# Seven products for half of an early first layer, and a transfer moved behind gathers, in an attention and expert-routing kernel

## The chip, the cores and the metric

One core of a Trainium2 chip runs the whole kernel. Its engines are TensorE (matmuls, PE in the profile), VectorE (DVE), ScalarE (ACT), GpSimd (POOL) and SyncE (SP, which here only issues transfers). The metric is the device time in microseconds of one execution, as the median of several; lower is better.

## The reference

Attention over blocks of 64 positions with a decaying state, then a routing layer in which each of 3072 tokens goes to one of 8 experts:

```python
batch, n_heads, seq, head_dim = (4, 8, 768, 64)
intra = einsum('bhic,bhjc->bhij', qb, kb) * Dmask        # per block of 64
out[:, :, sl] = einsum('bhij,bhjd->bhid', intra, vb) + einsum('bhid,bhde->bhie', qb * lam_pow, kv_state)
kv_state = lam_block * kv_state + einsum('bhsd,bhse->bhde', kb_dec, vb)
...
N, D, E, F = (3072, 512, 8, 1024)      # x: the attention's output, one row of 512 per token
logits = x @ w_gate
expert_idx = argmax(logits, axis=1)
gate_w = softmax(logits) at expert_idx
for e in range(E):
    h = maximum(x[mask] @ w1[e], 0.0)       # 512 -> 1024
    out[mask] = gate_w[mask] * (h @ w2[e])  # 1024 -> 512
```

All of it is in 32-bit floats.

## The kernel before

**Attention** runs in 12 steps of 128 positions and two batch rows. Each step turns q and k (L241), multiplies them (L279), applies the decay (L286), forms the output (L305, L314) and the state, turns the output back into token rows (L376), stores these in DRAM (`xs`, L386) and computes the logits (L366). From the logits VectorE finds each token's expert and its place in that expert's list; GpSimd stores the places one batch row at a time (L467, an indirect DMA into `slots`).

**Experts** are passes. Expert 5 (`FIRST`) comes in two parts: pass "0a" takes its first 256 tokens (`EARLY`) from the first four of the six blocks of positions and starts while the last step of the attention still runs; pass "0b" takes its other 128. Then follow the other seven experts, the second pass with up to 418 tokens. For each pass a list is read, its token rows are gathered from `xs` by an indirect DMA from GpSimd (`fetch`, L527, one per 128 tokens), turned so that features lie on partitions (`xgT`), and taken through w1 and w2. The two parts of expert 5 are turned by TensorE (`turn`, L592). From the second expert on, ScalarE splits the rows into 16-bit halves (`split`, L575, `planes_q` and `planes_k`), SP issues transposing DMAs (L577), and ScalarE joins the turned halves to `xgT` (`join`, L585).

**The layers.** Pass 0a's first layer (`hidden`, L606) is plain: for each of 8 blocks of 128 hidden features 4 matmuls of 128x128 weights with 256 tokens, then a ReLU by ScalarE (L559). Its second layer (`outputs_early` and `form_early`, matmuls in `block`, L774) multiplies hT by w2 as a 2x2 matrix of blocks with seven products instead of eight (Strassen's method in Winograd's form): with sums s1 to s4 of blocks of hT (`left_of`, L752 to L755, tiles h_qT, h_kT, h_sd, h_kd) and t1 to t4 of blocks of w2 (`second_sums`, L683, tiles t_q, t_k, t_v, t_m), both by VectorE, and u2, u3, u4 as running sums of products. Pass 0b has a plain first layer (128 tokens) and a second layer of seven products in halves of the array (`lone_tile`, L782, its adds L819 to L832). From the second expert on both layers use seven products (`hidden_fast`, L728, with sums of w1 by GpSimd in `first_sums`, L655 and L652, and sums of xgT by VectorE in `token_sums`, L713; `outputs_across`, L914).

**What sets the order.** Each engine takes its instructions in the order written out by the program; a scheduler places those that aren't pinned (`pin`). An engine waits on semaphores at an instruction, and what stands behind that instruction waits with it. Products lie in 8 banks of the accumulator memory (`bank(i, ...)`): a product in a bank waits until the engine that read the previous product there has done so. Tiles come from pools with a few buffers for each name (`qkv`: 3, `work`: 2, `wpool`: 2); xgT and hT have one buffer each.

**Around the end of the attention** GpSimd gathers pass 0a (`gather_early`), then waits until TensorE has turned back the last logits (`hold`), stores the last six places, and then gathers 0b and the second expert. SP loads w2 of expert 5 behind the early gathers, the lists, and w1 of the second expert (`load_weights`). Two tiles of the old state are reused as space: `qs_room` has four parts, `x_room` two.

## Time and profile before

| | |
|---|---|
| median of 3 runs | 434.31 us (432.14 to 435.08) |
| profiled execution | 435.07 us, of it a span of 432.8 us |
| busy: PE, DVE, POOL, ACT | 421.3, 266.0, 257.5, 176.8 us |
| granted TensorE clock, mean | 0.997 |
| DMA | 83.49 MB, mean 193 GB/s |

Times in the trace count from the start of the span. A row of the timeline is start, length, engine, line, operation, output<-inputs, and in brackets the idle time ahead of it and what ended that. Lxxx is a line of the kernel. Each matmul in 32-bit floats stands in the trace as two records. The chain of waits follows the work that ended last back to its start; "issue" in it is time in which the engine waited for nothing that the profile shows. In the table by stages stand, after the stage and its length, the busy times of PE, PE's weight loads, DVE, ACT and POOL with their counts, the clock, the share of the DMA engines and GB/s.

### The profile page before, as it was taken

To read this page: it belongs to the slowest core of one execution; us is meant where nothing else is said; L and a number is where in the kernel's file an instruction comes from. 1 tells how busy PE (TensorE), PEld (TensorE's weight loads), DVE (VectorE), ACT (ScalarE), POOL (GpSimd) and SP (SyncE) were. 2 spreads that over 40 slices of the span, in tenths; PEclk is the share of its full clock that TensorE was granted. 3 is DMA by queue.
4 is the path that set the end of the run, shared out by engine and by line. 5 is a ranking of instruction groups with operands and counts; after the bars stand their busy time and mean duration, and the time that the engine had idled before them with its cause. 6 is when DMAs were issued, how large, how long until landed. Compare 5 with 4: busy or idle time off the path is not lost.

```text
span 432.8 us, 9573 instructions
## 1 busy us (share of the span) xinstructions
PE 421.3 (97%) x3699; PEld 393.9 (91%) x3699; DVE 266.0 (61%) x585; ACT 176.8 (41%) x319; POOL 257.5 (59%) x205
## 2 busy tenths in 40 slices
PE   8999999999999999999999999999999999999993
PEld 6888898888888897999999999999999999999972
DVE  6656656566766647686547757755575664775463
ACT  3366545555542423450554155245424605422221
POOL 5243457373344368777948757693885887749032
PEclk9999999999999999999999999999999999999998
DMA  9999989999985758976369857965975894753122
GB/s 174 211 245 229 220 213 213 233 193 249 292 283 149 265 105 234 325 246 237 52 139 190 332 76 157 319 179 112 299 246 81 196 384 80 153 186 56 20 83 63
DMA packets 164727, 83.49 MB, mean 193 GB/s; under 512 B 146019, under 2 KB 146063, under 8 KB 164672
## 3 DMA queue, kind: packets, MB, share of 16 engines
q1 hardware_dynamic: 155024, 63.21, 61.2%
q0 software_dynamic: 5712, 13.26, 10.2%
q10 hardware_dynamic: 3936, 6.31, 4.2%
q8 instruction: 31, 0.51, 0.5%
q14 instruction: 24, 0.20, 0.2%
HBM read 58.96 MB, written 13.09 MB: 166 GB/s over the span
## 4 chain that ended last, share of the span: by engine, by line
PE 87%; DMA 4%; issue 3%; ACT 2%; POOL 1%; SPq 1%; DVE 1%; POOLq 0%; ACTq 0%
PE p L728 30%; PE p L914 26%; PE sp L279 5%; PE ph L606 5%; PE op L314 4%; PE p L774 3%; DMA v_in<-in_v_dram 3%; PE cp L340 2%; PE tx L376 2%; PE tk L241 2%; PE tq L241 2%; PE op L305 2%; PE p L782 2%; PE lgT L366 1%; DMA xg<-xs,list_0a 1%
## 5 line engine op out<-in xcount | busy, mean ns | idle before, releaser
L533 POOL DMA_INDIRECT out_dram<-o_room,list x24 | 25.7, 1069 | 51.9 <-DMA decay<-planes_q 22.4
L286 DVE TENSOR_TENSOR mt<-sp,decay 128x512 f32<-128x512 f32 x48 | 30.1, 684 | 23.8 <-PE sp L279 18.6
L739 ACT ACTIVATE hT<-hT 128x418 f32<-128x418 f32 (+6 forms) x56 | 28.3, 521 | 34.1 <-DVE hT L736 31.2
L728 PE MATMUL p<-xgT,w1t 128*128 128x209 f32 (+6 forms) x224 | 41.4, 327 | 0.0
L728 PEld LDWEIGHTS p<-xgT,w1t 128*128 128x128 f32 x224 | 37.1, 189 | 0.8 <-issue 0.8
L618 ACT COPY u_qT<-p 128x418 f32<-128x418 f32 (+6 forms) x14 | 6.7, 479 | 69.5 <-PE p L728 69.5
L914 PE MATMUL p<-hT,w2t 128*128 128x209 f32 (+5 forms) x192 | 33.6, 328 | 0.0
L914 PEld LDWEIGHTS p<-hT,w2t 128*128 128x128 f32 x192 | 32.0, 189 | 0.0
L467 POOL DMA_INDIRECT slots<-entry,slot_i x24 | 23.8, 990 | 13.1 <-PE tl L391 5.9
L527 POOL DMA_INDIRECT xg<-xs,list x25 | 25.9, 1034 | 9.0 <-issue 6.1
L736 DVE TENSOR_TENSOR hT<-p,u_kd 128x418 f32<-128x418 f32 (+6 forms) x28 | 15.6, 559 | 21.0 <-PE p L728 21.0
L279 PE MATMUL sp<-qT,kT 64*128 64x128 f32 x384 | 27.5, 293 | 0.4 <-ACT kT L263 0.4
L279 PEld LDWEIGHTS sp<-qT,kT 64*128 64x128 f32 x384 | 24.3, 199 | 3.0 <-issue 2.0
L269 POOL TENSOR_TENSOR kd<-k_in,kdec 128x512 f32<-128x512 f32 x12 | 12.4, 1042 | 23.7 <-PE cp L340 11.9
L655 POOL TENSOR_TENSOR s_q<-w1t 128x1024 f32<-128x1024 f32 x7 | 16.5, 2363 | 16.6 <-DVE t_xT L713 14.6
L326 ACT COPY xT<-op 128x512 f32<-128x512 f32 x12 | 7.0, 585 | 36.9 <-PE op L314 33.8
L606 PE MATMUL ph<-xgT,w1t 128*128 128x256 f32 (+1 forms) x128 | 21.6, 328 | 0.0
L606 PEld LDWEIGHTS ph<-xgT,w1t 128*128 128x128 f32 x128 | 19.2, 191 | 1.7
L728 PE MATMUL p<-t_sd,w1t 128*128 128x209 f32 (+6 forms) x112 | 20.7, 327 | 0.0
L728 PE MATMUL p<-st,s_q 128*128 128x209 f32 (+6 forms) x112 | 20.7, 327 | 0.0
L652 POOL TENSOR_TENSOR w1t<-w1t 128x1024 f32<-128x1024 f32 x7 | 20.2, 2892 | 0.6
L728 PE MATMUL p<-t_xT,w1t 128*128 128x209 f32 (+6 forms) x112 | 20.6, 326 | 0.0
(252 smaller groups left out, 1093.9 us busy)
## 6 DMA issues: line engine op xcount, KB each, us to landing
w2t<-in_moe_w_dram SPq DMA_DIRECT2D x8, 2048.0 KB
w1t<-in_moe_w_dram SPq DMA_DIRECT2D x7, 2048.0 KB
xs<-x_room ACTq DMA_DIRECT2D x12, 512.0 KB
v_in<-in_v_dram SPq DMA_DIRECT2D x8, 512.0 KB
o_room<-qs_room SPq DMA_DIRECT2D x76, 48.0 KB
q_in<-in_q_dram SPq DMA_DIRECT2D x7, 512.0 KB
k_in<-in_k_dram SPq DMA_DIRECT2D x7, 512.0 KB
room<-in_q_dram SPq DMA_DIRECT2D x4, 512.0 KB
```

The lines of the kernel that those rows point to most:

```text
L241: pin(nc.tensor.transpose(t[:, i, b, :], src[:, b, h:h + 2, :], ident))
L279: m.scored = pin(nc.tensor.matmul(sp[u][:, i, b, :], lhsT=m.kT[s][halves[u], i, b, :], rhs=m.qT[s][halves[u], i, b, :], start=(i == 0 and ...
L286: nc.vector.tensor_mul(mt[:, u], sp[u], decay[:, u, s * HP // 2:(s + 1) * HP // 2].unsqueeze(2).to_broadcast(shp))
L314: pin(nc.tensor.matmul(out_at(m, b, u, hp), lhsT=m.v[:, b, 2 * hp + u, :], rhs=m.mt[hp // 2][:, u, hp % 2, b, :], start=(first and hp == 0 ...
L467: put = nc.gpsimd.indirect_dma_start(out=slots, out_offset=bass.IndirectOffsetOnAxis(ap=slot_i[:, i:i + 1], axis=0), in_=entry[:, n, bs[i] ...
L527: return nc.gpsimd.indirect_dma_start(out=dst, out_offset=None, in_=xs[:rows, :], in_offset=bass.IndirectOffsetOnAxis(ap=idx, axis=0))
L533: put = nc.gpsimd.indirect_dma_start(out=out, out_offset=bass.IndirectOffsetOnAxis(ap=idx, axis=0), in_=src, in_offset=None, bounds_check= ...
L606: nc.tensor.matmul(ph, lhsT=w1t[:, dc, fc * P:(fc + 1) * P], rhs=m.xgT[:, dc, :], start=(dc == 0), stop=(dc == DC - 1))
L652: return nc.gpsimd.tensor_tensor(out=o, in0=x, in1=y, op=ALU.add)
L728: nc.tensor.matmul(p[:, i, :], lhsT=lhs[:, dc, g, i * P:(i + 1) * P], rhs=rhs[:, dc, :], start=(dc == 0), stop=(dc == DH - 1))
L739: pin(nc.scalar.activation(outs[i][k], outs[i][k], ACT.Relu))
L914: nc.tensor.matmul(p[:, c, :], lhsT=lhs[:, f, c * P:(c + 1) * P], rhs=rhs[:, f, :], start=(f == 0), stop=(f == FC // 2 - 1))
```

## The change

Three things change between the end of the attention and the second expert.

*Pass 0a's first layer* (`hidden_early`). Hidden features 0 to 511 stay plain, 4 blocks of 4 matmuls with 256 tokens. Features 512 to 1023 become a 2x2 by 2x2 product: the weights' blocks have 256 input by 256 hidden features, the tokens' 256 by 128. Seven products of 4 matmuls (128x128 weights, 128 tokens). The four sums of w1 (`early_sums`, tiles e_q, e_k) are made by GpSimd right behind the early gathers, ahead of its last stores; the four sums of xgT (e_sd twice, st, e_xT) by VectorE ahead of the sums of w2, which are now interleaved with the adds of the products (`others`). ScalarE copies the first product out and applies the ReLUs. The third product is added onto the first in its bank.

*Pass 0a's second layer* (`outputs_early`). The same seven products in another order and with fixed banks: 7, 4, 5, 7, 4, 7, 4. The product a22 t4 comes third instead of last, the one of s4 last. The first product is copied out by ScalarE instead of VectorE. One of the two scatters is issued before the last product.

*Transfers.* The second expert's list is read before 0b's, its four gathers are issued before 0b's, and the load of its w1 waits until the second of these gathers has landed (`behind`). 0b's turned rows go to the third part of `qs_room` (`short_room`) instead of the xgT buffer.

```diff
-    def load_weights(e, later=None):
+    def load_weights(e, later=None, behind=None):
         w1t = wpool.tile([P, DC, F], F32, tag="w1", name="w1t")
-        nc.sync.dma_start(out=w1t, in_=pick(w1_r, e))
+        begun = nc.sync.dma_start(out=w1t, in_=pick(w1_r, e))
+        if behind is not None:
+            pin(begun)
+            tc.add_manual_dep(begun.ins, behind.ins.name, ...)
...
+    def early_sums(w1t):
+        w = w1t.rearrange("p (j d) (g i f) -> p i j d g f", j=2, g=2, i=2)
+        a = [[w[:, i, j, :, 1] for j in range(2)] for i in range(2)]
+        q, k = (qkv.tile([P, 2, DH, FH // 2], F32, tag=t, name=f"e_{t}") for t in "qk")
+        s1, s2, s3, s4 = q[:, 0], q[:, 1], k[:, 0], k[:, 1]
+        pin(pool_sub(s3, a[0][0], a[1][0]))
+        pin(pool_add(s1, a[1][0], a[1][1]))
+        pin(pool_sub(s2, s1, a[0][0]))
+        pin(pool_sub(s4, a[0][1], s2))
...
+    def hidden_early(m, w1t, a, others):
+        h = m.n // 2
+        m.hT = ffn.tile([P, FC, m.n], F32, tag="hT", name="hT", bufs=1)
+        for fc in range(FC // 2):
+            ph = bank(next(ph_banks), [P, m.n], "ph")
+            for dc in range(DC):
+                nc.tensor.matmul(ph, lhsT=w1t[:, dc, fc * P:(fc + 1) * P], rhs=m.xgT[:, dc, :],
+                                 start=(dc == 0), stop=(dc == DC - 1))
+            relu(1, m.hT[:, fc, :], ph)
...
+        x1 = product(a.a11, b.b11, 0)
+        pin(nc.scalar.copy(p1, x1))
+        x7 = product(a.s2, b.t2, 1)
+        ready(0, 0, product(a.a12, b.b21, 0, x1))
+        others.pop(0)()
+        add(u2, x7, p1)
+        x3 = product(a.s3, b.t3, 2)
+        others.pop(0)()
+        add(u3, x3, u2)
+        x6 = product(a.a22, b.t4, 3)
+        others.pop(0)()
+        add(outs[1][0], x6, u3)
+        ready(1, 0)
+        x5 = product(a.s1, b.t1, 6)
+        add(outs[1][1], x5, u3)
+        ready(1, 1)
+        add(u4, x5, u2)
+        others.pop(0)()
+        add(outs[0][1], product(a.s4, b.b22, 1), u4)
+        ready(0, 1)
...
+        for make in (a.s1_made, a.s2_made, a.s3_made, a.s4_made):
+            make()
+        nc.scalar.copy(p1, block(a.a11, b.b11, 7))
+        give(0, 0, block(a.a12, b.b21, 4), p1)
+        p6 = block(a.a22, b.t4, 5)
+        add(u2, block(a.s2, b.t2, 7), p1)
+        add(u3, block(a.s3, b.t3, 4), u2)
+        give(1, 0, p6, u3)
+        p5 = block(a.s1, b.t1, 7)
+        give(1, 1, p5, u3)
+        add(u4, p5, u2)
+        scatter(at(m, 1)[1], o[1])
+        ahead()
+        give(0, 1, block(a.s4, b.b22, 4), u4)
+        scatter(at(m, 0)[1], o[0])
...
         begun = fetch(m, 1 + (NSTEP - 2) * B * C, pin)
         hold(begun[0], other)
+        m.sums = early_sums(weights[0][0])
...
-    passes.append(make_pass(FIRST, EARLY, CAPS[0] - EARLY, "0b"))
     next_pass(1)
+    passes.insert(1, make_pass(FIRST, EARLY, CAPS[0] - EARLY, "0b"))
+    short_room = qs_room[:, 2].rearrange("p i b c -> p (i b) c")
     later = []
-    weights.append(load_weights(passes[2].w, later))
-    for m in passes[1:]:
-        fetch(m)
+    begun = fetch(passes[2], pin=pin)
+    fetch(passes[1], pin=pin)
+    weights.append(load_weights(passes[2].w, later, begun[1]))
```

On ScalarE, from the ReLUs of pass 0a to the copies that follow the split of the second expert's rows (`planes`), before:

```order
L559 ACTIVATE hT<-ph 128x256 x8
L575 COPY planes_q<-xg 128x512 x4
L575 COPY planes_k<-xg 128x512 x2
L575 COPY planes_k<-xg 48x512 x2
L599 COPY xgT<-tp 128x256
```

and now (`pe` are the products of the first layer's half, `x_room` holds the copy of the first product of the second layer):

```order
L564 ACTIVATE hT<-ph 128x256 x4
L671 COPY u_qT<-pe 128x256
L668 ACTIVATE hT<-pe 128x2x128
L668 ACTIVATE hT<-hT 128x2x128 x3
L580 COPY planes_q<-xg 128x512 x4
L580 COPY planes_k<-xg 128x512 x2
L580 COPY planes_k<-xg 48x512 x2
L867 COPY x_room<-p 128x256
```

Four of the eight ReLUs have become a copy and four ReLUs of a quarter each, and a copy of the second layer's first product stands behind the split.

On TensorE, the same stretch, the first and second layer of pass 0a, before:

```order
L606 MATMUL ph<-xgT,w1t 128x256 x28
L774 MATMUL p<-w2t,hT 128x256 x8
L774 MATMUL p<-t_k,h_kT 128x256 x4
L774 MATMUL p<-t_v,h_sd 128x256 x4
L774 MATMUL p<-t_q,h_qT 128x256 x4
L774 MATMUL p<-w2t,h_kd 128x256 x4
L592 MATMUL tp<-ident,xg 128x128 x4
L774 MATMUL p<-t_m,hT 128x256 x4
```

and now:

```order
L640 MATMUL ph<-xgT,w1t 128x256 x12
L658 MATMUL pe<-xgT,w1t 128x128 x4
L658 MATMUL pe<-st,e_q 128x128 x4
L658 MATMUL pe<-xgT,w1t 128x128 x4
L658 MATMUL pe<-e_sd,e_k 128x128 x4
L658 MATMUL pe<-e_xT,w1t 128x128 x4
L658 MATMUL pe<-e_sd,e_q 128x128 x4
L658 MATMUL pe<-xgT,e_k 128x128 x4
L836 MATMUL p<-w2t,hT 128x256 x8
L836 MATMUL p<-t_m,hT 128x256 x4
L836 MATMUL p<-t_k,h_kT 128x256 x4
```

Sixteen matmuls of 256 columns have become seven times four of 128, and the product with t_m has moved from the end of the second layer to its third place, ahead of the one (t_k, h_kT) that takes bank 7 again.

On GpSimd, from the early gathers on, before:

```order
L527 DMA xg<-xs,list_0a 128x512 x2
L1064 MEMSET between 128x1
L467 DMA slots<-entry,slot_i 27648x4
...
L467 DMA slots<-entry,slot_i 27648x4 x2
L527 DMA xg<-xs,list_0b 128x512
L527 DMA xg<-xs,list_2270 128x512 x3
L527 DMA xg<-xs,list_2270 48x512
```

and now (list_2270 and list_2274 are both the second expert's):

```order
L532 DMA xg<-xs,list_0a 128x512 x2
L717 TENSOR_TENSOR e_k<-w1t 128x512
L714 TENSOR_TENSOR e_q<-w1t 128x512
L717 TENSOR_TENSOR e_q<-e_q,w1t 128x512
L717 TENSOR_TENSOR e_k<-w1t,e_q 128x512
L1137 MEMSET between 128x1
L472 DMA slots<-entry,slot_i 27648x4
...
L472 DMA slots<-entry,slot_i 27648x4 x2
L532 DMA xg<-xs,list_2274 128x512 x3
L532 DMA xg<-xs,list_2274 48x512
L532 DMA xg<-xs,list_0b 128x512
```

Four sums have come between the early gathers and the last stores, and 0b's gather has moved behind the second expert's four.

More of the change, by code (lines that the diff above doesn't have):

```diff
@@ L198, in nothing @@
         pass
-    def load_weights(e, later=None):
+    def load_weights(e, later=None, behind=None):
         w1t = wpool.tile([P, DC, F], F32, tag="w1", name="w1t")
-        nc.sync.dma_start(out=w1t, in_=pick(w1_r, e))
+        begun = nc.sync.dma_start(out=w1t, in_=pick(w1_r, e))
+        if behind is not None:
+            pin(begun)
+            tc.add_manual_dep(begun.ins, behind.ins.name, mybir.DependencyInfo(
+                mybir.DependencyClass.Sync, mybir.DependencyReason.DATA),
+                reason="the gathers have the DMA engines first")
         w2t = wpool.tile([P, FC, MD], F32, tag="w2", name="w2t")
@@ L585, in join, with turn @@
             pin(nc.scalar.copy(to[:, u], m.across[u][:, :, :m.n]))
-    def turn(m, pin=lambda inst: inst):
-        m.xgT = ffn.tile([P, DC, m.n], F32, tag="xgT", name="xgT", bufs=1)
+    def turn(m, pin=lambda inst: inst, room=None):
+        m.xgT = room
+        if room is None:
+            m.xgT = ffn.tile([P, DC, m.n], F32, tag="xgT", name="xgT", bufs=1)
         for c in range(0, DC, 2):
@@ new lines, in hidden_early, with product, add, ready @@
+    def hidden_early(m, w1t, a, others):
[7 more added lines that the diff above has]
+            relu(1, m.hT[:, fc, :], ph)
+        b = [[m.xgT[:, j * DH:(j + 1) * DH, k * h:(k + 1) * h] for k in range(2)] for j in range(2)]
+        t1, t3, t4 = (work.tile([P, DH, h], F32, tag=t, name=f"e_{t}", bufs=n)
+                      for t, n in (("sd", 2), ("sd", 2), ("xT", 1)))
+        t2 = st.rearrange("p b g d -> p (b g d)")[:, :DH * h].rearrange("p (c n) -> p c n", c=DH)
+        b = right_sums(b, t1, t2, t3, t4, vector_sub)
+        p1, u2, u3 = thirds(h)
+        u4 = work.tile([P, 2, h], F32, tag="kT", name="u_4")
+        c = FC // 2
+        outs = [[m.hT[:, c + 2 * i:c + 2 * i + 2, k * h:(k + 1) * h] for k in range(2)]
+                for i in range(2)]
+        def product(lhs, rhs, at, onto=None):
+            p = bank(at, [P, 2, h], "pe") if onto is None else onto
+            for i in range(2):
+                for dc in range(DH):
+                    pin(nc.tensor.matmul(p[:, i, :], lhsT=lhs[:, dc, i * P:(i + 1) * P],
+                                         rhs=rhs[:, dc, :], start=(onto is None and i == dc == 0),
+                                         stop=(i == 1 and dc == DH - 1),
+                                         skip_group_check=True))
+            return p
+        def add(*x):
+            pin(nc.vector.tensor_add(*x))
+        def ready(i, k, src=None):
+            pin(nc.scalar.activation(outs[i][k], outs[i][k] if src is None else src, ACT.Relu))
+        x1 = product(a.a11, b.b11, 0)
[18 more added lines that the diff above has]
+        ready(0, 1)
@@ L790, in pair_rooms, with outputs_early @@
         return o, outs, [u[:, i, :] for i in range(4)]
-    def outputs_early(m, w2, ahead):
+    def outputs_early(m, b, ahead):
         a = left_of(m.hT, 0, P, pair_rooms_of_sums())
-        for make in (a.s3_made, a.s1_made, a.s2_made, a.s4_made):
-            make()
-        o, outs, temps = pair_rooms()
+        o, outs, (p1, u2, u3, u4) = pair_rooms()
+        add = nc.vector.tensor_add
         def give(i, k, p, u):
@@ L802, in give @@
                                            op0=ALU.mult, op1=ALU.add)
-        form_early(block, (a, w2), temps, give, ahead)
-        for i in range(2):
-            scatter(at(m, i)[1], o[i])
+        for make in (a.s1_made, a.s2_made, a.s3_made, a.s4_made):
[13 more added lines that the diff above has]
+        scatter(at(m, 0)[1], o[0])
     def lone_tile(m, i, b, banks):
@@ L1286 @@
         if i == 0:
-            w2 = second_sums(w2t, vector_sub)
-        if i < 2:
+            others = []
+            w2 = second_sums(w2t, lambda *x: others.append(lambda: vector_sub(*x)))
+            hidden_early(m, w1t, m.sums, others)
+        elif i < 2:
             hidden(m, w1t)
@@ L1308 @@
         if i == 0:
-            outputs_early(m, w2, lambda: turn(passes[1], pin))
+            outputs_early(m, w2, lambda: turn(passes[1], pin, short_room))
         elif i == 1:
```

14 lines of the change are left out of this document (1 added, 13 removed).

## The prediction

> **What bounds the kernel now.** I read the chain of waits first, from the early gather (tokens of expert 5 stored up to then) to the second expert. Columns: start, length, engine and line.
>
> ```profile
> 119.02 3.63 DMA xg<-xs,list_0a
> ...
> 127.81 12.19 PE ph L606 x56
> 140.00 10.36 PE p L774 x48
> 150.36 0.44 PE tp L592 x4
> 150.80 1.73 PE p L774 x8
> 152.53 7.14 PE ph L606 x64
> 159.67 6.11 PE p L782 x48
> 165.78 0.55 PE p L728 x2
> 166.33 0.35 issue
> 166.68 1.08 PE p L782 x8
> ```
>
> From 127.81 every piece but one is TensorE's own work: the early tokens' first layer (L606, 256 columns), their second layer (L774), the transposes of the rest of that expert ("0b"), its first layer (L606, 128 columns), its second (L782), then the second expert (L728). The exception is 0.35 us. TensorE's waits from 124 us to the end, and its stages later on:
>
> ```profile
> PE p L782 <- issue: 0.3, 1, 0.3
> ```
> ```profile
> 190.00:240.00 50.00, 50.00 (x290) 50.00 (x289) 32.81 (x45) 20.63 (x28) 36.92 (x22) 1.00 0.70 186
> 240.00:300.00 60.00, 60.00 (x357) 60.00 (x357) 37.88 (x65) 23.65 (x40) 41.49 (x22) 1.00 0.70 190
> ```
>
> The second number after the stage is PE's busy time: all of it, at clock 1.00. So a microsecond that TensorE loses or gains between 125 and 167 us arrives at the end undiminished, and no other engine's time counts unless TensorE waits for it. (A matmul stands in the trace as two records.)
>
> **Part 1: the seven products.** The first half of the layer keeps 32 of the 64 records. The first 8 lie before 127.81, so 24 follow, each 12.19/56 = 0.218 us: done at 127.81 + 5.22 = 133.03. The other half is 7 products of 4 matmuls of 128x128x128, 56 records, where 32 of 256 columns were (6.97 us). The same shape is in the chain: 0b's first layer, 64 records in 7.14 us, 0.1116 each. 56 x 0.1116 = 6.25 us, done at 139.28 where 140.00 was: **-0.72 us**. A product with 128 columns thus pays only 2% over half of one with 256, and the eighth that is saved survives.
>
> [...]
>
> **Part 2: the sums that feed them.** GpSimd makes four of 128x512 behind the early gathers:
>
> ```profile
> L269 POOL TENSOR_TENSOR kd<-k_in,kdec 128x512 f32<-128x512 f32 x12 | 12.4, 1042 | 23.7 <-PE cp L340 11.9
> ```
> ```profile
> 119.02 0.97 POOL L527 DMA_INDIRECT xg<-xs,list_0a  x1 [0.31 <-issue]
> ...
> 125.96 1.00 POOL L467 DMA_INDIRECT slots<-entry,slot_i  x1 [5.85 <-PE tl L391]
> ...
> 137.96 1.54 POOL L527 DMA_INDIRECT xg<-xs,list_0b  x1 [4.67 <-DMA list_0b<-slots]
> 139.81 0.97 POOL L527 DMA_INDIRECT xg<-xs,list  x1 [0.30 <-issue]
> 141.08 0.95 POOL L527 DMA_INDIRECT xg<-xs,list  x1 [0.30 <-issue]
> 142.33 1.08 POOL L527 DMA_INDIRECT xg<-xs,list  x1 [0.30 <-issue]
> ...
> 154.32 2.40 POOL L655 TENSOR_TENSOR s_k<-w1t 128x1024 f32<-128x1024 f32 x1
> ```
>
> 4 x 1.04 = 4.2 us fit into the 5.85 that GpSimd waits for TensorE there: cost nothing. What is queued behind them are the last stores of places, then the lists, then all gathers; without the cover, each microsecond past 125.96 would move these. VectorE makes four sums of 128x256 after 131.1 (its last row before the wait below) and then those of w2:
>
> ```profile
> 130.98 0.16 DVE L1254 TENSOR_REDUCE beyond<-beyond 128x1 int32<-128x8 int32 x1
> 133.90 1.23 DVE L683 TENSOR_TENSOR t_q<-w2t 128x1024 f32<-128x1024 f32 x1 [2.77 <-DMA w2t<-in_moe_w_dram]
> ...
> 137.43 1.22 DVE L683 TENSOR_TENSOR t_m<-w2t,t_k 128x1024 f32<-128x1024 f32 x1
> ...
> 142.51 0.42 DVE L633 COPY x_room<-p 128x256 f32<-128x256 f32 x1
> ...
> 145.22 0.42 DVE L635 TENSOR_TENSOR x_room<-p,x_room 128x256 f32<-128x256 f32 x1 [1.08 <-issue]
> ```
>
> At 0.42 each the first four lie in the 2.77 us wait: nothing. Then the four of w2 (133.90 to 138.65, 4.75 us) are interleaved with six adds of the products (6 x 0.42): the last is done at 133.9 + 4.75 + 2.5 = 141.2. TensorE needs that quarter of hT only in the third product of the second layer: 139.28 + 2 x 1.73 = 142.73 (8 records of L774 are 10.36/6 = 1.73). Nothing again.
>
> **Part 3: the copy of the first product of the second layer.** Before, VectorE copied it (L633). Now ScalarE does, and in ScalarE's order it stands behind the last ReLU and behind the eight copies that split the second expert's rows into halves. Those wait for gathers. Four blocks later TensorE takes bank 7 again, which that copy must have emptied: a wait that was not there. When TensorE gets there: 139.28 + 3 x 1.73 = 144.46. When the copy is done:
>
> ```profile
> 140.04 0.38 ACT L559 ACTIVATE hT<-ph 128x256 f32<-128x256 f32 x1 [1.34 <-PE ph L606]
> 146.70 2.18 ACT L575 COPY planes_q<-xg 128x512 uint16<-128x512 uint16 x4 [6.28 <-DMA xg<-xs,list]
> 148.99 2.18 ACT L575 COPY planes_k<-xg 128x512 uint16<-128x512 uint16 x4
> 151.08 0.36 ACT L599 COPY xgT<-tp 128x256 f32<-128x256 f32 x1
> ```
>
> From below: every gather has landed when the last ReLU is over, at 141.2 + 0.38 = 141.55. The eight copies take 146.70 to 151.17, 4.47 us, and the copy 0.36 (the row of L599, same shape): 146.4. From above by the nearest row of a gather: the early one, 3.63 us from issue to landing beside other loads. The second expert's four now go first; their list is issued in the slot of the one at 135.15, so I put them at the four starts 137.96 to 142.33. The last lands at 142.33 + 3.63 = 145.96, its two copies take 1.1, the bank is free at 147.4. TensorE waits 1.95 to 2.95 us. Neither row is nearer (the engines are emptier now, the last gather has 48 of 128 rows), so I take the middle: **+2.45 us**. The remaining four blocks and the transposes follow without a gap: VectorE's adds of 0.42 to 0.5 fit into blocks of 1.73.
>
> **Part 4: w1 of the second expert behind the gathers.** SP now issues it when the second gather has landed, about 139.81 + 3.63 = 143.4, not at 136.83:
>
> ```profile
> 135.15 0.34 SPq L496 DMA_DIRECT2D list_0b<-slots  x1
> 136.16 0.39 SPq L496 DMA_DIRECT2D list<-slots  x1
> 136.83 0.38 SPq L202 DMA_DIRECT2D w1t<-in_moe_w_dram  x1
> 147.35 1.32 SPq L577 DMA_TRANSPOSE decay<-planes_q  x1
> ```
> ```profile
> 139.00:140.00 1.00, 1.00 (x6) 0.90 (x5) 0.26 (x1) 0.00 (x0) 0.69 (x2) 1.00 1.02 410
> 146.00:147.00 1.00, 1.00 (x7) 0.87 (x6) 0.06 (x1) 0.30 (x1) 0.00 (x0) 1.00 0.97 356
> 147.00:148.00 1.00, 1.00 (x6) 0.90 (x5) 0.96 (x3) 1.00 (x3) 0.00 (x0) 1.00 0.37 96
> ```
>
> In the last column (GB/s) w1 and the gathers moved together from 139 to 147. Moved by 6.6 us, w1 is there by about 153.5. Behind it on SP stand the transposes, free to start with the copies; GpSimd's first sum of w1 stood at 154.3 behind the scatters of the early rows, and the last scatter now ends with the last block. Cost nothing. The gain: the transposes start some 4 us sooner, and the turned rows have a room that 0b's no longer holds, so they are joined before 0b's layer ends instead of after it.
>
> ```profile
> 163.81 0.60 DVE L713 TENSOR_TENSOR t_sd<-xgT 128x418 f32<-128x418 f32 x1 [2.22 <-ACT xgT L585]
> ...
> 166.19 0.43 DVE L819 TENSOR_TENSOR u_t<-p,u_t 64x256 f32<-64x256 f32 x1
> ```
>
> The join (L585) held VectorE's sums of the second expert (L713), and behind these stands the add (L819) that empties bank 4 for the last products of 0b's second layer; it ended at 166.62, TensorE went on at 166.68. That is the 0.35 us at 166.33: **-0.35 us**. 0b's gather comes fifth, landing near 147.5; its transposes come at about 152. Nothing.
>
> **Sum.** -0.72 + 2.45 - 0.35 = **+1.4 us** (+0.9 to +1.9 by the two bounds). The profiled execution took 435.07 us, a span of 432.8 and 2.27 around it, so it would be 436.5; it was 0.76 above the median of the runs shown, 434.31 (432.14 to 435.08). Against that median: **435.7 us**, slower by 0.3%.
>
> **The rivals.**
> *The bank is free in time.* If the split is through ScalarE before 144.5, only the gains are left: -0.72 - 0.35 = -1.07, 433.2 us. For it: gathers land sooner without w1. Against it: 141.55 + 4.47 + 0.36 is late even with every row there. Chance 0.16, with all cases in which the wait is under a microsecond.
> *The gathers land as late as before.* The split's first gather was issued at 139.81 and let ScalarE go at 146.70, 6.9 us. If the last two keep that because w1 catches up with them, the last lands at 149.2, the copy ends at 150.7, TensorE waits 6.2: +5.1, 439.4 us. It decides once w1's data start before the fourth gather's; before, w1 was issued at 136.83 and the rate rose only in 139 to 140, so from 143.4 its data start near 145.5, when the fourth is nearly in. Chance 0.08.
> *The stores are held up.* GpSimd's sums wait for w1's second half or run longer than 5.85 us; stores, lists and gathers slide, and the copy with them: a microsecond each, 436.7 at one. Chance 0.05.
> *The change doesn't do what it says:* the seven products wait for their sums between them as long as the saved eighth, TensorE reaches the same block at 140.0 + 5.2, waits 0.72 less for the bank, and the sum is the same 435.7. It changes only where the time lies. Chance 0.06.
> My forecast has the remaining 0.65.
>
> **How the numbers follow.** About 1% (4.3 us) is what a measurement of this kernel tells from no change. Only the late gathers (0.08) cross it, less what they would cost in between: slower 0.06. Faster by 4.3 is four times all the gains: 0.01. The rest, 0.93, is within. The range runs from the case of the free bank, 433.2, less a little for the spread of the runs (433.0), to 437.9: the upper bound of the sum, the held stores, and a part of the late gathers.
>
> **What would show it.** Right: 56 records of 128 columns in about 6.3 us; a wait of TensorE of 2 to 3 us, with ScalarE's copy of the first block as what ended it, ahead of the block that reads the second sums of hT; no wait in 0b's second layer; GpSimd's next store still at about 126. Wrong: no wait there (the free bank), or one of 6 us with ScalarE idle for a gather (late gathers), or stores after 127.

## The result, and the profile after

The changed kernel took **439.18 us** (median of 6 runs, 437.81 to 442.38), the kernel before 434.14 beside it: a ratio of 1.0114, 95% interval 1.0078 to 1.0150. The forecast was 435.7, with 437.9 as its upper end. The direction was right, the size was not: +5.0 us instead of +1.4.

The profiled execution took 439.06 us, its span is 437.3 where the one of before was 432.8. Where these 4.5 us lie is read from the starts of TensorE's stages. Timeline of TensorE before (start, length, engine, line, operation): the early tokens' first layer, their second layer, 0b's transposes, 0b's second layer, the second expert's second layer.

```profile
125.51 1.46 PE L606 MATMUL ph<-xgT,w1t 128*128 128x256 f32 x6
...
139.84 3.62 PE L774 MATMUL p<-w2t,hT 128*128 128x256 f32 x16
...
150.20 0.60 PE L592 MATMUL tp<-ident,xg 128*128 128x128 f32 x4
...
159.60 1.08 PE L782 MATMUL p<-w2t,hT 128*64 128x256 f32 x4
...
187.56 2.99 PE L914 MATMUL p<-hT,w2t 128*128 128x209 f32 x16
```

The same timeline of the changed kernel, with the rows around the one wait (L658: the seven products; L836: blocks of the second layer).

```profile
124.48 1.46 PE L640 MATMUL ph<-xgT,w1t 128*128 128x256 f32 x6
...
131.90 1.05 PE L658 MATMUL pe<-xgT,w1t 128*128 128x128 f32 x8
...
138.15 3.62 PE L836 MATMUL p<-w2t,hT 128*128 128x256 f32 x16
141.60 1.89 PE L836 MATMUL p<-t_m,hT 128*128 128x256 f32 x8
147.66 3.78 PE L836 MATMUL p<-t_k,h_kT 128*128 128x256 f32 x8 [4.17 <-ACT x_room L867]
151.23 2.92 PE L836 MATMUL p<-t_v,h_sd 128*128 128x256 f32 x8
...
155.71 0.60 PE L599 MATMUL tp<-ident,xg 128*128 128x128 f32 x4
...
165.11 1.08 PE L844 MATMUL p<-w2t,hT 128*64 128x256 f32 x4
...
192.00 2.99 PE L987 MATMUL p<-hT,w2t 128*128 128x209 f32 x16
```

| stage | before | after | difference |
|---|---|---|---|
| start of the early tokens' first layer | 125.51 | 124.48 | -1.03 |
| their first layer | 14.33 | 13.67 | -0.66 |
| their second layer up to 0b's transposes | 10.36 | 17.56 | +7.20 |
| 0b's transposes and first layer | 9.40 | 9.40 | 0.00 |
| 0b's second layer, second expert's first | 27.96 | 26.89 | -1.07 |
| up to TensorE's last matmul | 238.28 | 238.28 | 0.00 |

The first row is how the attention happened to go in these two executions (in all profiles told of here this start lies between 123.0 and 127.2). The whole loss is in the third, and 4.17 of it is one wait. TensorE's waits from 110 us to the end:

```profile
PE p L836 <- ACT x_room L867: 4.2, 1, 4.2
PE tp L599 <- DMA xg<-xs,list_0a: 0.9, 2, 0.6
```

The other 3.03 us have no wait: the three blocks behind it took 3.78, 2.92 and 1.89 us where the block ahead of the wait took 1.89. The table by stages says why (busy times of PE, its weight loads, DVE, ACT, POOL, then the clock):

```profile
145.00:146.00 1.00, 0.00 (x0) 0.00 (x0) 0.00 (x0) 0.34 (x1) 0.00 (x0) 1.00 0.94 369
146.00:147.00 1.00, 0.00 (x0) 0.00 (x0) 0.00 (x0) 0.80 (x2) 0.00 (x0) 0.73 0.96 393
147.00:148.00 1.00, 0.34 (x1) 0.34 (x2) 0.35 (x1) 0.60 (x2) 0.00 (x0) 0.50 1.01 406
...
153.00:154.00 1.00, 1.00 (x6) 0.86 (x5) 0.00 (x0) 0.00 (x0) 0.00 (x0) 0.85 1.25 256
```

TensorE stands from 143.49. A mean of 0.73 in the microsecond from 146 means a clock of 1.00 up to 146.46 and 0.50 from there: it fell 3.0 us into the wait, and came back at about 153.3, when TensorE had worked for 5.6 us again, 6.8 us at half in all. Half of these 5.6, 2.8 us, is all but 0.2 of the 3.03. In the trace of before the clock was at 1.00 up to TensorE's last matmul and at 0.50 only in the idle end: its last matmul ended at 425.84, and a mean of 0.56 in the microsecond from 430 puts the fall at 430.1. None of its waits, 1.1 us at the longest, had the half clock behind it; the working left that out.

Who made the wait: ScalarE's timeline; then GpSimd's last sum of w1, its next store, and its gathers for the second expert and 0b, with one row of VectorE between them; then the chain of waits at the fourth gather.

```profile
139.72 0.42 ACT L668 ACTIVATE hT<-hT 128x256 f32<-128x256 f32 x1 [1.38 <-DVE hT L665]
...
146.20 1.14 ACT L580 COPY planes_k<-xg 48x512 uint16<-48x512 uint16 x2 [0.86 <-DMA xg<-xs,list]
147.24 0.36 ACT L867 COPY x_room<-p 128x256 f32<-128x256 f32 x1
```
```profile
121.91 1.28 POOL L717 TENSOR_TENSOR e_k<-w1t,e_q 128x512 f32<-128x512 f32 x1
...
124.93 1.00 POOL L472 DMA_INDIRECT slots<-entry,slot_i  x1 [1.70 <-PE tl L396]
...
137.22 0.97 POOL L532 DMA_INDIRECT xg<-xs,list  x1 [4.77 <-DMA list<-slots]
...
138.14 1.22 DVE L745 TENSOR_TENSOR t_m<-w2t,t_k 128x1024 f32<-128x1024 f32 x1
...
138.49 1.69 POOL L532 DMA_INDIRECT xg<-xs,list  x1 [0.30 <-issue]
140.49 1.19 POOL L532 DMA_INDIRECT xg<-xs,list  x1 [0.31 <-issue]
141.99 0.96 POOL L532 DMA_INDIRECT xg<-xs,list  x1 [0.30 <-issue]
143.25 0.96 POOL L532 DMA_INDIRECT xg<-xs,list_0b  x1 [0.30 <-issue]
```
```profile
141.99 4.19 DMA xg<-xs,list
```

The copy of the first product waits in ScalarE's queue for the fourth gather, as the prediction had it; TensorE waited 1.2 us longer than the prediction's upper bound. The four sums ended at 123.19, and the next store began 0.45 us after the start of the first layer, as before (125.96 and 125.51).

### The profile page after: what moved, and what is told of

Read it like the earlier page. It is cut to its first block, busy times and chain, and to the rows that moved or that the text cites. A ratio compares the mean times of both kernels' runs of the same rounds, so it can differ in the third digit from the quotient of the medians.

```text
span 437.3 us, 9647 instructions
## 1 busy us (share of the span) xinstructions
PE 422.3 (97%) x3723; PEld 396.0 (91%) x3723; DVE 270.4 (62%) x594; ACT 178.0 (41%) x321; POOL 263.6 (60%) x209
## 4 chain that ended last, share of the span: by engine, by line
PE 89%; DMA 4%; issue 1%; POOL 1%; ACT 1%; DVE 1%; SPq 1%; POOLq 0%; DVEq 0%
PE p L790 29%; PE p L987 25%; PE sp L284 6%; PE p L836 5%; PE op L319 4%; PE p L844 3%; PE tx L381 3%; PE cp L345 3%; PE tk L246 2%; PE op L310 2%; PE tq L246 2%; PE ph L613 2%; PE lgT L371 1%; DMA xg<-xs,list_0a 1%; DMA xg<-xs,list 1%
## 5 line engine op out<-in xcount | busy, mean ns | idle before, releaser
L532 POOL DMA_INDIRECT xg<-xs,list x25 | 27.4, 1095 | 11.2 <-issue 6.0
L790 PE MATMUL p<-xgT,s_v 128*128 128x209 f32 (+6 forms) x112 | 20.5, 326 | 0.0
L790 PE MATMUL p<-xgT,s_k 128*128 128x209 f32 (+6 forms) x112 | 20.5, 326 | 0.0
```

Of the source, the lines that this page charges most:

```text
L532: return nc.gpsimd.indirect_dma_start(out=dst, out_offset=None, in_=xs[:rows, :], in_offset=bass.IndirectOffsetOnAxis(ap=idx, axis=0))
L790: nc.tensor.matmul(p[:, i, :], lhsT=lhs[:, dc, g, i * P:(i + 1) * P], rhs=rhs[:, dc, :], start=(dc == 0), stop=(dc == DH - 1))
```

## The experiments

**The copy and the clock.** Four kernels take the changed kernel's wait apart. The first gives the copy to VectorE, as it was before:

```diff
-        nc.scalar.copy(p1, block(a.a11, b.b11, 7))
+        nc.vector.tensor_copy(p1, block(a.a11, b.b11, 7))
```

> The changed kernel with one edit: VectorE instead of ScalarE copies the first product of the second layer out of bank 7. Theory A (the copy's place behind the split, then the clock): VectorE reaches the copy at about 142.8 us, TensorE the bank at 143.4, so the wait of 4.2 us goes, and with it the half-speed stretch that followed (3.0 us): 439.2 - 7.2 = 432.0 us, or 433.0 by the forecast's own gains (-0.72 and -0.35 against 434.1). Rival B (the moved transfers: w1's load now falls on TensorE's blocks and on the gathers, the copy is a bystander): the slow blocks stay, 438 to 439 us.

The second leaves the wait and fills it with work in a bank that nobody uses:

```diff
         p6 = block(a.a22, b.t4, 5)
+        spare = bank(6, [P, m.n], "spare")
+        for k in range(8):
+            pin(nc.tensor.matmul(spare, lhsT=b.t4[:, k % 4, :P], rhs=m.hT[:, k, :], start=(k == 0), stop=(k == 7)))
```

> The changed kernel with 8 more matmuls of 256 columns (3.45 us), into a bank that nobody reads, ahead of the block that waits for bank 7; the copy stays where it is. Theory A: the wait up to about 147.6 us is the same, but TensorE is idle for 0.7 us of it only, its clock stays at 1.00, and the three blocks behind it take 1.73 us each instead of 8.2 us together: 439.2 - 3.0 = 436.2 us. Rival B (the traffic of w1 slows TensorE's reads): the blocks stay slow, 439 us.

The third keeps the copy on ScalarE and puts it ahead of the split's eight copies, by making the split a generator that stops ahead of each 128 rows; `rest()` runs what remains. The fourth has `range(4)` in place of `range(1)`, so the copy stands behind six of the eight:

```diff
-            split(passes[2])
+            parts = split_parts(passes[2])
+            for _ in range(1):
+                next(parts)
...
-        nc.scalar.copy(p1, block(a.a11, b.b11, 7))
+        pin(nc.scalar.copy(p1, block(a.a11, b.b11, 7)))
+        rest()
```

> The changed kernel with ScalarE's copy of the first product placed ahead of all eight copies of the split; ScalarE still makes it. Theory A: as with VectorE, 432.0 to 433.0 us; the split starts 0.4 us later, which the gathers hide. Should ScalarE itself be the trouble and not the place in its queue, or should rival B hold: 438 to 439 us.

> The changed kernel with ScalarE's copy placed behind six of the eight copies of the split, ahead of the two that wait for the fourth gather. Theory A: the copy ends at about 145.7 us, TensorE waits about 2.3 us, too short for the clock to fall (it fell 3.3 us into the wait of 4.2): 439.2 - 1.9 - 3.0 = 434.3 us. If instead the clock falls after any such wait, with a slow stretch in proportion, 435.8 us. Rival B: 438 to 439 us.

Measured: copy on VectorE 435.91 us, ratio 1.0033 (1.0004 to 1.0062); wait filled 437.02, 1.0078 (1.0048 to 1.0107), the clock at 1.00 throughout and 1.1 us of the wait left; copy first 435.45, 1.0031 (0.9999 to 1.0063); behind six of eight 437.34, 1.0063 (1.0028 to 1.0097). So by the medians the copy's place in the queue is worth some 3.5 us, and keeping the clock up through the wait 2.2 of them. (The intervals of the change and of the filled wait overlap; in their profiles the second layer's stage is 2.4 us shorter with the wait filled, 15.14 against 17.56.) The fourth kernel's wait and the chain behind it:

```profile
PE p L841 <- ACT x_room L872: 2.3, 1, 2.3
```
```profile
144.92 7.13 PE p L841 x24
```

24 records take 5.18 us by the 0.216 of before: 1.95 more behind a wait of 2.3 us, which I had expected to be too short for it, counting 3.3 us to the fall in the change where the trace has 3.0. The clock stood at half from 146.1 to 149.6 (means of 0.57 in the microsecond from 146 and 0.72 in the one from 149), and half of these 3.4 us is 1.7. But the first and third should have ended below the kernel before, at 432 to 433, and stood 1.7 and 1.3 us above it. Their chains have a new piece; the copy on VectorE:

```profile
142.47 7.65 DMA xg<-xs,list_0b
...
150.88 3.11 PE p L836 x8
```

0b's gather, now the fifth, lands 7.65 us after its issue; TensorE waits 2.7 us for it (2.2 with the copy first), and in this profile the next block pays half clock again, 3.11 instead of 1.73. In the changed kernel the longer wait at the copy had hidden this.

**0b's gather.** On top of "copy first", two kernels. One puts list and gather of 0b back to the front; w1 stays behind the second expert's second gather:

```diff
-    next_pass(1)
-    passes.insert(1, make_pass(FIRST, EARLY, CAPS[0] - EARLY, "0b"))
+    passes.append(make_pass(FIRST, EARLY, CAPS[0] - EARLY, "0b"))
+    next_pass(1)
...
-    begun = fetch(passes[2], pin=pin)
-    fetch(passes[1], pin=pin)
+    fetch(passes[1], pin=pin)
+    begun = fetch(passes[2], pin=pin)
```

> ScalarE's copy ahead of the split as in the run with the copy first, and the list and the gather of the short pass ahead of the second expert's, as in the kernel before; w1 still waits for the second expert's second gather. Theory A: in the runs with the copy out of the way the time was set by the short pass's gather, which went fifth, beside the w1 load, and landed 7.4 to 7.7 us after its issue; first in the queue it lands 3.5 to 4.5 us after its issue, some 4 us before TensorE comes for it, so the wait of 2.2 at its transposes goes and no clock falls behind it: 435.45 - 2.2 = 433.2, ratio to before 0.998. Rival B: the second expert's gathers, each about 1.2 us later, hold up the split and the join instead, and TensorE waits at the second expert's transposed rows: 435 again.

The other leaves the gathers and lets w1 wait for the fifth:

```diff
-    fetch(passes[1], pin=pin)
-    weights.append(load_weights(passes[2].w, later, begun[1]))
+    last_begun = fetch(passes[1], pin=pin)
+    weights.append(load_weights(passes[2].w, later, last_begun[-1]))
```

> The run with the copy first, with w1 waiting for the short pass's gather, the fifth, and not for the second one. Theory A: the short pass's gather landed 7.4 us after its issue because the 2 MB of w1 went beside it; without that it lands about 4 us after its issue, at about 146, before TensorE comes for it at 147, and the wait of 2.2 is gone. What is left then is the chain through SyncE's transposes and the third expert's gathers to GpSimd's sum s_q: w1, and the transposes queued behind it on SyncE, start 3 to 4 us later, so s_q comes later and TensorE waits for it 1 to 3 us in the second expert's first layer: 434.5 to 436. Rival B: w1's traffic has nothing to do with it, the fifth gather of a queue lands late in any case: a wait of some 2 us at the short pass's transposes stays.

Measured: 436.47 us, 1.0065 (1.0026 to 1.0104), and 439.7, 1.0107 (1.0072 to 1.0142). In both TensorE's wait for 0b's gather is gone. The DMA table of the second, with issue to landing in us:

```profile
xg<-xs,list_0b POOLq DMA_INDIRECT x1, 3.4
```

3.4 us without w1 beside it, 7.3 to 7.7 in the kernels with w1 beside it (in the changed kernel w1 was issued at 142.74, the gather at 143.25). With the copy first it was 7.4, and the place of w1 is the only edit between that kernel and this: the load made it late. The fourth gather felt the load too: ScalarE took up its rows 3.9 us after its issue with the copy first, and 3.5 us after at most with w1 behind all gathers. But neither kernel became faster, since TensorE now waited further on. The waits with 0b first:

```profile
PE p L795 <- POOL s_q L722: 2.7, 1, 2.7
PE p L849 <- DVE u_t L898: 1.0, 1, 1.0
```

s_q is GpSimd's third sum of the second expert's w1, for its first layer (L728 before, L795 here). It stands on GpSimd behind the third expert's four gathers; these wait for their list; the list is read by SP behind the second expert's eight transposes. No step of my working had this chain.

The same two profiles show that the length of a wait does not decide what the clock does. With 0b first the clock stayed at 1.00 through and behind the 2.7 us for s_q (from 166.46 to 169.12):

```profile
168.00:169.00 1.00, 0.00 (x0) 0.00 (x0) 0.00 (x0) 1.00 (x3) 1.00 (x1) 1.00 1.05 354
```

With w1 behind all gathers it fell for a wait of 1.8 us:

```profile
160.01 0.68 PE L849 MATMUL p<-t_v,qs_room 128*64 128x256 f32 x1 [1.83 <-DVE qs_room L819]
```
```profile
161.00:162.00 1.00, 1.00 (x8) 0.63 (x6) 0.21 (x1) 1.00 (x2) 0.00 (x0) 0.50 0.06 16
```

**The parts alone.** Four kernels. In the kernel before, the transfers' part of the change:

```diff
-    weights.append(load_weights(passes[2].w, later))
-    for m in passes[1:]:
-        fetch(m)
+    begun = fetch(passes[2], pin=pin)
+    fetch(passes[1], pin=pin)
+    weights.append(load_weights(passes[2].w, later, begun[1]))
...
-            outputs_early(m, w2, lambda: turn(passes[1], pin))
+            outputs_early(m, w2, lambda: turn(passes[1], pin, short_room))
```

> The kernel before with the transfers' part of the change alone (order of the lists and of the gathers, w1 behind the second gather, the short pass's rows in a room of their own); first layer and second layer as before. The prediction: the join comes earlier, -0.35, and the short pass's gather costs nothing: 433.8. Theory A: the short pass's gather lands 7.4 to 7.7 us after an issue at about 143.5, so at 151, and TensorE, which came for it at 150.2 in the kernel before, waits about 1 us at it: 434.9, ratio 1.002. Rival B: the w1 load, some 8 us later than before, is the late one and TensorE waits for it later: above 436.

In the kernel before, the sums of w1:

```diff
         hold(begun[0], other)
+        early_sums(weights[0][0])
```

> The kernel before with the four GpSimd sums behind the early gathers added, their results used by nothing. The prediction: they cost nothing, 434.2. Rival B: they hold back the early gathers, which land at 4.6 us after their issue and not at 3.6; TensorE's wait at the early tokens' transposes, 0.3 us in the kernel before, becomes about 1 us, and all behind it comes 0.7 us later: 434.9, ratio 1.002.

In the kernel before, these sums and the products that use them, with before's second layer:

```diff
-            w2 = second_sums(w2t, vector_sub)
-        if i < 2:
+            others = []
+            w2 = second_sums(w2t, lambda *x: others.append(lambda: vector_sub(*x)))
+            hidden_early(m, w1t, m.sums, others)
+        elif i < 2:
             hidden(m, w1t)
```

> The kernel before with the first layer's seven products and GpSimd's sums alone: lists, gathers, w1 and the second layer's blocks in their old order, its first copy on VectorE as before. The prediction: -0.72, so 433.2 to 433.5. Theory A, from the run with the products and the new order of blocks: TensorE reaches the second expert's first layer 0.7 earlier, but GpSimd's s_q, behind the third expert's gathers, does not come earlier; it waits 0.5 to 1 us for it, and nothing is gained: 433.9 to 434.5. Rival B: the products themselves make what is behind them late (VectorE's and GpSimd's work side by side stretches the gathers' issue): over 435.5, as the run with the new order of blocks.

And the kernel with the copy first, its transfers put back to what they were (the first diff of this part, reversed); it was profiled twice:

> The change with the transfers' part left as in the kernel before (lists, gathers and w1 in their old order) and ScalarE's copy ahead of the split. What is left is the first layer's seven products, the GpSimd sums and the second layer's new order of blocks. The prediction: seven products save 0.72, sums cost nothing: 433.5, ratio 0.998. Rival B: the GpSimd sums behind the early gathers make these land about 1 us later (4.6 against 3.6 us after issue), and TensorE's wait at the early tokens' transposes eats the 0.7: 434.2 to 434.6. Rival C: the gathers, late as in the kernel before, meet TensorE earlier, and it waits at the short pass's transposes: over 435.

> The products with the new order of blocks and the old transfers once more, for a second profiled execution: the first one took 433.87, the fastest of its ten, and the median was 437.4. Theory A: the profile shows TensorE's wait for GpSimd's s_q again, longer than the 0.9 of the first (2 to 3 us), and the clock at half behind it. Rival B: the time is lost ahead of the first layer, at the early tokens' gather (a wait of 2 us and the clock behind it).

Measured: transfers alone 435.64 us, 1.0029 (0.9989 to 1.0069), with waits where the theory had them; sums alone 434.44, 1.0002 (0.9966 to 1.0038); seven products 436.91, 1.0040 (1.0007 to 1.0073); products with the new order of blocks 437.38, 1.0065 (1.0026 to 1.0104). TensorE's waits with the transfers alone:

```profile
PE tp L599 <- DMA xg<-xs,list_0b: 1.2, 1, 1.2
PE p L735 <- POOL s_q L662: 0.8, 1, 0.8
```

SP's eight transposes began sooner with the transfers moved, but were not through sooner. The second of them before:

```profile
148.78 1.20 SPq L577 DMA_TRANSPOSE across<-planes_q  x1
```

and in the changed kernel, beside w1's load:

```profile
145.07 3.68 SPq L582 DMA_TRANSPOSE across<-planes_q  x1
```

Counted from the start of the first layer, the first transpose was issued 3.1 us sooner in the changed kernel and the last 0.2 later; with the transfers alone 2.7 sooner and 1.5 later.

The sums are free, as forecast, within 0.4%. The transfers alone gain nothing. The products, which save 0.7 on TensorE, made the kernel slower in both versions. In the seven products TensorE comes to 0b's second layer 0.5 us sooner than before, counted from the start of the first layer, but s_q ends 0.8 later (44.04 against 43.28), and TensorE waits 1.1 us for it. That GpSimd's issues get longer beside VectorE's sums was rival B of this run, and its 435.5 or more is what was measured; in the profile of these products with s_q ahead (below) GpSimd took 6.07 us to issue 0b's gather and the next three, and 4.54 before. With the new order of blocks the first profile, of the fastest of ten executions (433.87 us), shows a wait of 0.9 for s_q; the second, of a single execution, took 439.67 us. Its waits, its GpSimd, and its clock:

```profile
PE p L795 <- POOL s_q L722: 3.0, 1, 3.0
```
```profile
163.12 1.21 POOL L532 DMA_INDIRECT xg<-xs,list  x1 [5.53 <-DMA list<-slots]
...
168.04 2.37 POOL L722 TENSOR_TENSOR s_q<-w1t 128x1024 f32<-128x1024 f32 x1
```
```profile
168.00:169.00 1.00, 0.00 (x0) 0.00 (x0) 0.94 (x3) 0.00 (x0) 0.99 (x2) 1.00 1.01 348
169.00:170.00 1.00, 0.00 (x0) 0.00 (x0) 0.12 (x1) 0.84 (x2) 1.00 (x1) 0.66 0.99 367
170.00:171.00 1.00, 0.53 (x2) 0.52 (x3) 0.00 (x0) 1.00 (x3) 0.92 (x2) 0.50 1.05 350
```

The third expert's gathers began 2.1 us later than in the first profile, counted from the start of the first layer, for their list; the wait grew by as much and took the clock with it, until 176.1. The kernel before has no room there either, and its trace says so. GpSimd and TensorE before:

```profile
166.41 2.38 POOL L655 TENSOR_TENSOR s_q<-w1t 128x1024 f32<-128x1024 f32 x1
...
168.86 1.66 PE L728 MATMUL p<-st,s_q 128*128 128x209 f32 x8
```

s_q is done at 168.79, its product begins at 168.86. TensorE was on time to within 0.1 us; what it saves ahead of this place it waits for here, unless s_q comes sooner too.

**The sum out of the way.** In the two profiles of the products GpSimd idles 3.4 and 5.5 us ahead of the third expert's gathers, and s_q takes 2.4. So in four kernels it (s2 in the code) goes ahead of them, for the second expert alone: the products with the new order of blocks, the kernel before, the whole change with the copy first, and the seven products.

```diff
         pin(pool_add(s1, a[1][0], a[1][1]))
+        if ahead_of_gathers:
+            pin(pool_sub(s2, s1, a[0][0]))
```

> The products with the new order of blocks and the old transfers, with one thing moved: GpSimd's sum s_q of the second expert's w1 stands ahead of the third expert's gathers and not behind them. In the two profiles without the move GpSimd stood idle 3.4 and 5.5 us ahead of these gathers, for their list; the sum takes 2.4, so it fits, and the gathers lose nothing. Theory A: TensorE's wait for s_q (0.9 and 3.0 us in those profiles, with the clock at half behind the 3.0) is what ate the products' gain; it is gone now, and the time is 437.4 - 0.9 to 6 = some 433.3, 0.7 below before, ratio 0.998. Rival B: the wait for s_q was a symptom, and the next thing on the same chain, VectorE's sums of the joined rows, holds TensorE up at the same place: 436 to 437.

> The kernel before with s_q ahead of the third expert's gathers and nothing else changed. Theory A: in the kernel before s_q ends 43.3 us behind the start of the early tokens' first layer and TensorE comes for it about 0.5 later, so that in most executions nothing is gained: 434.0, ratio 1.000; where the list comes late (its landing varied by 2 us between two profiles) there is a gain, so 433.3 to 434.2. Rival B: s_q beside VectorE's and ScalarE's work there slows these: over 435.

> The whole change with ScalarE's copy ahead of the split, and with s_q ahead of the third expert's gathers. Theory A: the wait for s_q was hidden there behind the 2.2 us that TensorE waits for the short pass's gather, which stays; so most of the time stays too, 435.45 without the move: 434.5 to 435.4. Rival B: a good part of the 1.3 above before was s_q in executions that no profile shows: 433.5 or less.

> The seven products and GpSimd's sums in the kernel before, the second layer's blocks and the transfers in their old order, with s_q ahead of the third expert's gathers. Theory A: the wait for s_q (1.1 us in the profile without the move) is gone and the products' 0.72 comes through, but for what the early tokens' gather costs where it lands late: 433.3 to 434. Rival B: what is lost is lost ahead of the first layer (that profile waited 2.5 us for the early tokens' gather and ran its transposes at half clock, and had begun 2 us earlier than others): 436 as without the move.

Measured: 434.61 us, 1.0001 (0.9972 to 1.0030), where the same kernel without the move had 1.0065; 434.24, 1.0002 (0.9975 to 1.0028); 437.72, 1.0059 (1.0023 to 1.0095); 435.60, 1.0028 (0.9996 to 1.0061). With the new order of blocks the move brings back the 0.6%, so there s_q was what it cost; in the kernel before it changes nothing. In the seven products 1.0040 became 1.0028, which is no distinction, so how much of their loss is s_q stays open. In the whole change nothing was gained: 0b's gather (2.2 us) is still there, and more was lost than I had expected. All four profiles have a new wait of 1.1 to 1.3 us for VectorE. GpSimd and VectorE in the first:

```profile
156.27 2.36 POOL L722 TENSOR_TENSOR s_q<-w1t 128x1024 f32<-128x1024 f32 x1
...
157.12 1.78 DVE L822 TENSOR_TENSOR qs_room<-hT 128x256 f32<-128x256 f32 x1
158.83 0.41 DVE L823 TENSOR_TENSOR qs_room<-hT 128x256 f32<-128x256 f32 x1
```

VectorE's sum for 0b's second layer starts beside s_q and takes 1.78 us, its equal behind it 0.41. The last kernel makes s_q (`finish.first`) wait for the last of VectorE's four sums, still ahead of the gathers:

```diff
         for make in (t.s3_made, t.s1_made, t.s2_made, t.s4_made):
-            make()
+            made = make()
+        finish.first(made)
+        gathers()
```

> As the products with s_q ahead of the third expert's gathers, but s_q waits for VectorE's four sums of the short pass. In the run without this wait VectorE's first sum took 1.78 us, not 0.41, and ended 0.3 behind s_q, which ran beside it; TensorE waited 1.1 for it. Theory A: GpSimd's and VectorE's sums of this kind do not run side by side, so VectorE's sum is back at 0.4, TensorE's wait there is gone, and s_q, over some 2.3 later, is still there when TensorE comes for it; from the start of the early tokens' first layer to the second expert's second layer it takes 62.2 - 1.1 = 61.1 us in the profile, where the kernel before took 62.05; the time 433.5, 0.8 below before. Rival B: VectorE's 1.78 has another reason, or the third expert's gathers, a microsecond later, are the next wait: 434.6 and a span of that stretch over 62.

```profile
158.82 0.41 DVE L825 TENSOR_TENSOR qs_room<-hT 128x256 f32<-128x256 f32 x1
...
160.64 2.38 POOL L722 TENSOR_TENSOR s_q<-w1t 128x1024 f32<-128x1024 f32 x1 [2.58 <-DVE qs_room L828]
```

Measured: 434.00 us, 1.0005 (0.9975 to 1.0036). VectorE's sum is back at 0.41 and the wait is gone. So the 1.78 us came with s_q beside the sum, the inputs of both in tiles; why the one holds up the other was not shown. VectorE's adds that take one input from a bank took 0.42 to 0.43 us beside s_q in the kernel before (L821 to L826): they were not held up. Another 0.5 us then goes to VectorE's u_t. The time does not tell this kernel from the one before, and no version here beats it.

One measure sets the profiles side by side without the attention's variation: the stretch from the start of the early tokens' first layer to the start of the second expert's second layer, from the same two rows as in the table above. Each row is one execution, and several were faster than their kernel's median (copy first 432.83 us, 0b first 434.91, products with the new order 433.87). The last column is how long the clock stood at half within the stretch; the 0.8 of the seven products lies at its start (six records of the first layer in 1.84 us, 1.46 in the change), behind waits of 1.0 and 1.5 us for the early gather ahead of it.

| kernel | stretch, us | TensorE's largest waits in it, us | half clock, us |
|---|---|---|---|
| before | 62.05 | | |
| the change | 67.52 | copy 4.2 | 6.8 |
| copy on VectorE | 65.04 | 0b's gather 2.7 | 3.4 |
| wait filled | 65.11 | copy 1.1 | |
| copy first | 62.76 | 0b's gather 2.2 | |
| copy behind six of eight | 64.74 | copy 2.3 | 3.4 |
| copy first, 0b first | 64.44 | s_q 2.7, u_t 1.0 | |
| copy first, w1 behind all gathers | 66.52 | s_q 2.0, qs_room 1.8 | 3.4 |
| transfers alone | 63.50 | 0b's gather 1.2, s_q 0.8 | |
| sums alone | 62.04 | u_t 0.3 | |
| seven products | 62.60 | s_q 1.1 | 0.8 |
| products, new order of blocks; again | 62.52; 67.23 | s_q 0.9; 3.0 | none; 6.8 |
| the same, s_q ahead | 62.21 | qs_room 1.1 | |
| the same, s_q behind VectorE's sums | 61.54 | u_t 0.5 | |
| before, s_q ahead | 62.87 | qs_room 1.3 | |
| copy first, s_q ahead | 64.29 | 0b's gather 2.2, qs_room 1.3 | |
| seven products, s_q ahead | 62.23 | qs_room 1.3 | |

## Why the prediction was wrong, step by step

- **Part 1, -0.72.** The duration was right: seven products from 131.90 to 138.15, 6.25 us as forecast, and the layer 0.66 shorter. That a gain "arrives at the end undiminished" was wrong. It was argued from busy shares and the list of waits of before, which show that TensorE waits for nothing worth naming, but not how much room it has. The room at s_q was under 0.1 us, to be read from two rows that I did not set side by side.
- **Part 2, nothing.** Right as a cost: the sums alone measure 1.0002. They ran 1.27 to 1.31 us each and not 1.04, and still ended ahead of the next store. The profiles with the sums show TensorE waiting 0.6 to 2.5 us for the early gather; of those without, before's lists no such wait, the other two 0.7 and 1.0. The early gather landed 4.3 us after its issue with the transfers alone, which has no such sums, and 4.4 with the copy first, which has them, so a landing of that length needs no sums; whether the sums have a part in the longer waits stays open.
- **Part 3, +2.45: the step that failed.** Mechanism, engine and place were right, the size was not: 4.17 us, where the bounds were 1.95 and 2.95. TensorE came when forecast: 143.49 is 19.0 us after its first layer began, and so was the forecast's 144.46 on before's count. The copy was 1.3 us later than the upper bound, on the same count. The first gather was issued 0.3 later. The first three issues took 3.85 us together, not 3.46; the longest, 1.69, ran beside VectorE's t_m and ended 0.8 behind it (140.18 against 139.36). The fourth gather landed 4.19 after issue, not 3.63, in part because of w1's load behind it (the 3.9 and 3.5 us above, with it and without). The upper bound rested on one landing, that of the early gather, and I took the middle below it.
- **What Part 3 left out, +3.03.** TensorE's clock fell to half in this wait and stayed there for 5.6 us of work. This term is larger than the one forecast and was in no sum, range or rival; without it 4.17 in place of 2.45 gives 437.4 us, inside the range. Filling the wait with work took 2.2 us off.
- **Part 4, -0.35 and "Nothing".** The stage in which the 0.35 lay did become 1.07 shorter. The turned rows were joined 1.6 us sooner, counted from the start of the first layer, but TensorE also came 6.5 us later; with the copy first these are 1.0 and 1.8 for the same stage of 26.89. How much of the 1.07 is the one and how much the other stays open. The transfers alone gained nothing: there the join came 0.2 sooner, since the transposes started sooner but were not through sooner, and the stage was 27.97, with a wait of 0.8 for s_q in it. "0b's gather ... Nothing" was wrong: it landed 7.3 to 7.7 us after issue beside w1, and costs 1.2 to 2.7 us as soon as the copy does not hide it. Both errors have the same root: a 2 MB load was moved, and only its own landing and SP's queue were followed, not what it slows.
- **The rivals.** Late gathers stood at 439.4 us, next to what was measured, but by a wait of 6.2 us behind a landing at 149.2; the landing was 146.18, or 147.2 on before's count. The load of w1 did make the fourth gather later, as this rival had it, but it took 4.2 us from issue to landing and not 6.9, and the half clock made up the rest: the number agrees by chance. The free bank, the held stores and the products waiting for their sums are ruled out by the rows above.

By stages: -0.66 + 4.17 + 3.03 - 1.07 = +5.5 us in the profiled stretch, +5.0 in the medians.

## What to carry to other kernels

Before a gain on the busiest engine is counted, look up when each operand that it meets further on is ready: "no waits" in a profile can mean much room or none, and here TensorE had less than 0.1 us of it. Price a new wait on TensorE as long as those here with a chance of the half clock behind it, 1.7 to 3.0 us: of nine waits of 1.8 to 4.2 us in these stretches five had it. When a load is moved, list what now runs beside it, gathers above all: 0b's landed after 7.4 us beside w1 and after 3.4 without it.

## What the runs showed of the hardware

- In the stretches of the table TensorE's clock fell to one half in or behind waits of 1.8, 2.3, 2.7, 3.0 and 4.2 us, and not for waits of 2.0, 2.2, 2.2 and 2.7 us. It stayed at half for 3.4 us in three of the five (copy on VectorE, six of eight, w1 behind all gathers) and for 6.8 in two (the change, the products again), part of it in the wait, which cost 1.7 to 3.0 us. So the length alone did not decide: a wait of 1.8 us was enough once (w1 behind all gathers), and one of 2.7 was not (0b first). What else does was not shown; no run here moved a wait without changing its length.
- An indirect gather of 128 rows (0b's) landed 3.4 us after its issue with no load beside it, and 7.3 to 7.7 us after it in the seven profiles with the gather fifth and a load of 2 MB beside it (issued 0.51 us ahead in the changed kernel, 0.55 with the copy first, 0.07 with the transfers alone).
- The first of VectorE's sums for 0b's second layer, 128x256 of two tiles, took 1.78 us beside GpSimd's s_q (products with s_q ahead) and 1.96 (before, s_q ahead), and 0.41 without it (before, and s_q behind VectorE's sums).
- In the profiles of before and of the change, between 112 and 175 us, GpSimd's issue of an indirect DMA took 0.86 to 1.04 us, but for six of 1.07 to 1.69, and each of these six had a VectorE sum of two tiles beside it. Not each issue beside such a sum was longer (0.97 at 139.81 and 0.95 at 141.08 in before, 0.96 at 141.99 in the change). No run here moved a sum alone to test that.
